# Gates of two feed-forward steps computed together, and a planner that orders shared PSUM reads

## The chip, the cores and the metric

The kernel runs on one core of a Trainium2 chip. The metric is the device time of one execution in microseconds (us). The core has engines that run side by side, each through its own list of instructions in order: TensorE (matmuls into PSUM; PE in the profile, PEld its weight loads), VectorE (DVE), ScalarE (ACT), GpSimd (POOL, hardly used here) and SyncE (SP, which here only issues DMAs).

## The reference

Attention in a sliding window of 64 positions over 8 batches, 8 heads, 576 positions and heads of 64, and behind it a feed-forward layer whose activation is a rational function:

```python
scores = scale * q @ k.T            # only 0 <= rel < 64 counts
attn = softmax(scores)
x = (attn @ v)  ->  [4608 tokens, 512]
h = x @ w_in                        # [4608, 2048]
P = a[0] + a[1] * h + a[2] * h**2 + a[3] * h**3
Q = 1.0 + abs(b[0]) * abs(h) + abs(b[1]) * h**2
out = (P / (Q + 1e-06)) @ w_out     # [4608, 512]
```

## The kernel before, in words

**Tiles and stages.** The tokens are cut into 12 chunks of CH = 384. For a chunk, four attention *units* (one for two heads each; `unit_load`, `unit_scores`, `unit_soft`, `unit_norm`, `unit_transpose`, `unit_av`, lines 402 to 513) produce x, transposed, as a high and a low part. A *step* (c, i) is chunk c and block i of 128 of the 2048 hidden columns; there are 12 x 16 = 192 steps, in the order of `phases` (line 545): the first two chunks take the first half of the blocks and then the second, so that the weights can arrive meanwhile, and all later chunks take 16 blocks in a row.

**A step.** `ffn1` (line 517) multiplies x by a block of w_in: 12 matmuls of 384 columns into one PSUM tensor h, of which there are two in turn. Then comes the gate (lines 529 to 543): ScalarE reads h three times (Square into u, Abs into r, Identity into num), VectorE reads it twice (num times h, then num plus a1, times h); after that h is free. From u, r and num alone follow u (the denominator less one), Ln and Exp on ScalarE (its reciprocal, in r), the quotient gh, rounded for TensorE, and the remainder gl, through u, u and gl on VectorE. `ffn2` (line 550) multiplies gl and gh by blocks of w_out: nine matmuls of 512 columns into the three PSUM tensors o. It stands LAG = 3 steps behind `ffn1`, and its first matmul reads gl. The rings: r, u and num two tiles each, gh and gl GB = 4 each.

**Weights.** `load_weight` (line 370) turns one staged load w_st into a high and a low part: ScalarE writes top, VectorE puts c (tile w_c) together, ScalarE casts c to the high part, VectorE subtracts to the low part. The loads pass through six spare slots and then a ring of SLOTS = 3; after each conversion `fetch` issues the next load.

**The order of the work.** Nothing runs in the order in which it is written. Every call is recorded by a `Planner` (lines 51 to 226) with a cost, an issue time (`occ`) and a latency (`own`), and the operations it must follow by overlap of what they read and write. `plan` (line 183) then plays a list schedule: the engine that can start first takes, of its operations that are ready, the one that was recorded first. The instructions are emitted in the order of these planned starts, which fixes each engine's list; the waits between engines follow from the emitted order. Because all instructions come out of `emit`, they all stand at line 226 in the profile, and one goes by the names of tiles. `fill` (line 210) puts warming matmuls into gaps that TensorE has before the first use of o.

**Attention units.** The scores go into the PSUM pair ps_s; in chunks up to ON_PE = 2 the mask is added by TensorE, later by VectorE. The softmax is written to sm (ring of two), multiplied by the reciprocal sums on VectorE, transposed by TensorE into ps_s, and copied to pT (one tile) by ScalarE. The products with v go to ps_x. The loads qk and vt have rings of two.

Of the kernel before, what the change touches and what calls it, by code (L numbers as in the profile page):

```python
# [9 lines left out]
F32 = mybir.dt.float32  # L10
# [11 lines left out]
CH = 384  # L22
# [3 lines left out]
LAG = 3  # L26
GB = 4
SLOTS = 3
WARM = 7
FILL = 430  # L30
C1AT = 0, 0, 1, 3
ON_PE = 2
# [18 lines left out]
class Planner:  # L51
# [4 lines left out]

    def __init__(self, nc, free, shares):
        self.nc, self.shares = nc, shares
        self.ops, self.group_op = [], None
        self.free = dict(free)  # L60
        self.hist, self.known, self.loads = {}, {}, []
        for name, engine in dict(vector="DVE", scalar="ACT", tensor="PE", gpsimd="POOL", sync="SP").items():
            setattr(self, name, Recorder(self, engine, getattr(nc, name)))
# [46 lines left out]
    def cost(self, engine, method, out, reads, kw, args):  # L110
        if isinstance(out, Late):
            n = out.size // 4
        else:
            n = 1
            for _, k in out.ap[1:]:
                n *= k
        if engine == "SP":
            parts = 128 if isinstance(out, Late) else (out.ap[0][1] if out.tensor.__class__.__name__ != "DRamTensorHandle" else 0)
            size = mybir.dt.size(out.dtype) * n * (parts or out.ap[0][1])
            return 400, 400, size  # L120
        if engine == "PE":
            if method == "transpose":
                return 109, 270, 0
            if isinstance(args[2], Late):
                n = args[2].size // 4
            else:
                n = 1
                for _, k in args[2].ap[1:]:
                    n *= k
                if args[2].dtype == F32:  # L130
                    return (45, 270, 0) if args[1].ap[0][1] == 64 else (52, 225, 0)
            return n * 0.452, n * 0.452 + 165, 0
        if engine == "ACT":
            if "accum_out" in kw:
                return 343, 450, 0
            f = args[2] if len(args) > 2 else None
            occ = 58 + 0.813 * n
            if n == 512:
                occ = 640 if method == "copy" and getattr(out, "dtype", None) == F16 else 510
            for k in ("scale", "bias"):  # L140
                if isinstance(kw.get(k), bass.AP):
                    occ += 92
            if f in (AF.Ln, AF.Exp):
                occ += 55
            return occ, occ + 120, 0
        if engine == "DVE":
            if method == "tensor_reduce":
                n = 1
                for _, k in reads[0].ap[1:]:
                    n *= k  # L150
            if n < 16:
                return 90, 185, 0
            occ = 65 + 1.045 * n
            if isinstance(kw.get("scalar"), bass.AP):
                occ += 62
            return occ, occ + 85, 0
        if engine == "POOL":
            return (n * 2.0 + 60, n * 2.0 + 100, 0) if method in ("tensor_scalar", "tensor_copy") else (n * 2.4 + 130, n * 2.4 + 170, 0)

    def add(self, op):  # L160
        op.index, op.before, op.after = len(self.ops), set(), []
        op.ready = max([self.known.get(name, 0) for name, *_ in op.reads + op.writes], default=0)
        for is_write, spans in ((False, op.reads), (True, op.writes)):
            for name, p0, p1, b0, b1 in spans:
                for q0, q1, c0, c1, other, wrote in self.hist.get(name, ()):
                    if (wrote or is_write) and p0 < q1 and q0 < p1 and b0 < c1 and c0 < b1:
                        op.before.add(other)
# [6 lines left out]
        for wrote, spans in ((False, op.reads), (True, op.writes)):  # L174
            for name, p0, p1, b0, b1 in spans:
                h = self.hist.setdefault(name, [])
                if wrote:
                    h[:] = [x for x in h if not (p0 <= x[0] and x[1] <= p1 and b0 <= x[2] and x[3] <= b1)]
                h.append((p0, p1, b0, b1, op.index, wrote))
                if name in self.shares:  # L180
                    self.hist.setdefault(self.shares[name], []).append((0, 128, 0, 1 << 20, op.index, False))

    def plan(self):
# [6 lines left out]
        for _ in self.ops:  # L190
            start, engine = min((max(self.free[e], min(o.ready for o in w)), e) for e, w in waiting.items() if w)
            op = min((o for o in waiting[engine] if o.ready <= start), key=lambda o: o.index)
            waiting[engine].remove(op)
# [35 lines left out]
class Recorder:  # L229
# [3 lines left out]
    def __getattr__(self, method):  # L233
        return lambda *args, **kw: self.planner.record(self.engine, self.owner, method, args, kw)


# [11 lines left out]
def swa_rational_ffn(ctx: ExitStack, tc: tile.TileContext, qk, v, w_in, w_out, out):  # L248
# [56 lines left out]

    warm = const.tile([P, 512], BF16, name="warm")
    nc.vector.memset(warm, 0.0)
    for _ in range(WARM):
        nc.tensor.matmul(ps_o[2], warm[:, 0:P], warm, start=True, stop=True)
    make_mask()  # L310
# [28 lines left out]
    UNIT = QKAB + TC * P  # L339
    qk_ring = Ring(ring, 2, [P, QKAB], F32, "qk")  # L340
    vt_ring = Ring(ring, 2, [P, TC * P], F32, "vt")
    w_ring = Ring(ring, SLOTS, [P, 1026], F32, "w_st")
    spare = [late.tile([P, H * NCC * P], F32, name=f"early_{n}", tag=f"late_{n}") for n in ("wi_h", "wi_l")]
    spare_slots = [t[:, k * 1026:(k + 1) * 1026] for k in range(H * NCC * P // 1026) for t in spare]
    c_ring = Ring(ring, 2, [P, 512], F32, "w_c")
    top_ring = Ring(const, 0, [], F32, "top")
    top_ring.tiles = tops
    sm_ring = Ring(ring, 2, [P, 2, PR, P], F32, "sm")
    pT_ring = Ring(ring, 1, [P, 2, PR * P], F32, "pT")
    small = {n: Ring(ring, 2, [P, 2 * PR], F32, n) for n in ("nmx", "sums", "rs")}  # L350
    tmp = {n: Ring(ring, 2, [P, CH], F32, n) for n in ("r", "u", "num")}
    g_ring = [Ring(ring, GB, [P, CH], F32R, n) for n in ("gh", "gl")]
    ob_ring = Ring(ring, 2, [P, DO], F32, "ob")

    shares = {t.tensor.name: f"late_{n}" for t, n in zip(early + spare, ("wo_l", "wo_h", "wi_h", "wi_l"))}
    pl = Planner(nc, dict(DVE=4700, ACT=2100, PE=WARM * 430 + 1200, POOL=5000, SP=750), shares)
    pl.ready_at(mask, 4300)
# [12 lines left out]
    def load_weight(which, i):  # L370
        w = staged.pop((which, i))
        f = (lambda t: t.rearrange("p c n -> p (c n)")) if which == "in" else (lambda t: t)
        hi_name, lo_name = ("wi_h", "wi_l") if which == "in" else ("wo_h", "wo_l")
        top, c = top_ring(), c_ring()
        low = w.bitcast(U32)[:, 0:1024].rearrange("p (n two) -> p n two", two=2)[:, :, 1]
# [13 lines left out]
    def load_qk(c, hp):  # L389
        qk_t = early[hp // 2][:, hp % 2 * UNIT:hp % 2 * UNIT + QKAB] if c == 0 else qk_ring()  # L390
        pl.sync.dma_start(out=qk_t, in_=qk[hp, c])
# [48 lines left out]
    def score_maximum(c, hp):  # L440
        u = live[c, hp]
        on_pe, ps, both, m = u["on_pe"], u["ps"], u["both"], u["m"]
        sm, nmx = u["sm"], u["nmx"] = sm_ring(), small["nmx"]().rearrange("p (z r) -> p z r", z=2)
        if not on_pe:
# [30 lines left out]
    def unit_transpose(c, hp):  # L475
        u = live[c, hp]
        ps, both = two_banks(c, hp, True)
        with pl.group():
            for j in range(2 * PR):
                pl.tensor.transpose(ps[j // PR][:, (j % PR) * P:(j % PR + 1) * P], u["sm"][:, j, :], ident)  # L480
        pT = u["pT"] = pT_ring()
        if both is not None:
# [33 lines left out]

    def ffn1(c, i):
        h = h_ring()[:, 0:CH]
        n = 0
# [3 lines left out]
        with whole:  # L523
            for cc in range(NCC):
                with pl.group():
                    for w, x in (("wi_h", 1), ("wi_h", 0), ("wi_l", 0)):
                        pl.tensor.matmul(h, weight_piece(w, i, cc), x_sb[x_slot(c)][x][cc], start=n == 0, stop=n == 3 * NCC - 1)
                        n += 1
        r, u, num = (tmp[n]() for n in ("r", "u", "num"))
        gh, gl = (g() for g in g_ring)  # L530
        pl.scalar.activation(u, h, AF.Square)
        pl.scalar.activation(r, h, AF.Abs, scale=b_raw[:, 0:1])
        pl.scalar.activation(num, h, AF.Identity, scale=a_sb[:, 3:4], bias=a_sb[:, 2:3])
        pl.vector.scalar_tensor_tensor(out=u, in0=u, scalar=b_sb[:, 1:2], in1=r, op0=ALU.mult, op1=ALU.add)
        pl.scalar.activation(r, u, AF.Ln, bias=QADD)
        pl.scalar.activation(r, r, AF.Exp, scale=-1.0)
        pl.vector.tensor_tensor(out=num, in0=num, in1=h, op=ALU.mult)
        pl.vector.scalar_tensor_tensor(out=num, in0=num, scalar=a_sb[:, 1:2], in1=h, op0=ALU.add, op1=ALU.mult)
        pl.vector.scalar_tensor_tensor(out=gh, in0=num, scalar=a_sb[:, 0:1], in1=r, op0=ALU.add, op1=ALU.mult)
        pl.vector.scalar_tensor_tensor(out=u, in0=u, scalar=QADD, in1=gh.bitcast(F32), op0=ALU.add, op1=ALU.mult)  # L540
        pl.vector.scalar_tensor_tensor(out=u, in0=num, scalar=a_sb[:, 0:1], in1=u, op0=ALU.add, op1=ALU.subtract)
        pl.vector.tensor_tensor(out=gl, in0=u, in1=r, op=ALU.mult)
        gs[c, i] = gh, gl

    phases = [(0, 0, H), (1, 0, H), (1, H, NF), (0, H, NF)] + [(c, 0, NF) for c in range(2, NCH)]
    steps = [(c, i) for c, i0, i1 in phases for i in range(i0, i1)]
    total = len(steps)
    part = {}

    def ffn2(s):  # L550
# [89 lines left out]
    for s in range(total + LAG):  # L640
# [3 lines left out]
        if s < total:  # L644
            ffn1(*steps[s])
        for fn, *args in todo.get(s, ()):
# [4 lines left out]
    pl.plan()  # L651
    pl.fill("PE", ps_o[2].tensor.name, FILL, (nc.tensor.matmul, (ps_o[2], warm[:, 0:P], warm), dict(start=True, stop=True)))
    pl.emit()
# [37 lines left out]
```

## Time and profile before

| | us |
|---|---|
| median of 3 runs | 982.18 (982.14 to 982.31) |
| the profiled execution | 982.07 |
| its span, first to last instruction | 980.3 |
| TensorE busy | 952.6 (97%) |
| VectorE busy | 911.2 (93%) |
| ScalarE busy | 698.5 (71%) |
| DMA queue, share of 16 engines | 20.2% |

A row of a group reads: line, engine, operation, what it writes <- what it reads, shape, count | busy time in us, mean ns of one | idle time of the engine just before these instructions, and what ended it. A row of the timeline reads: start in us, length in us, engine, line, operation, tiles. Matmuls overlap: one takes 0.33 to 0.40 us in the rows, but the next one starts after 0.17 us (384 columns) or 0.23 us (512 columns). VectorE's and ScalarE's rows overlap a little as well, so what an instruction costs its engine is read from start to start. A row of the waits reads: who waited <- for whom: us in total, times, longest.

### The profile page before, as it was taken

The numbers are of one execution on the slowest core, as the hardware profiler recorded it, in microseconds if no ns is written. First come the engines' busy times: TensorE is split into PE (matmuls) and PEld (weight loads), VectorE is DVE, ScalarE is ACT, GpSimd is POOL, SyncE is SP. The second block draws the span as 40 slices with busy tenths as digits, with TensorE's granted clock in tenths as the row PEclk, the third lists the DMA queues.
The fourth block names the chain that finished last, engine by engine and source line by source line (L and its number), as shares of the span: only waits on it lengthen the run. The fifth ranks groups of instructions, "written<-read, shape, count | busy, mean of one in ns | idle before, by whom it ended". The sixth has DMA issues, their size and how long they took to land.

```text
span 980.3 us, 17701 instructions
## 1 busy us (share of the span) xinstructions
PE 952.6 (97%) x6672; PEld 824.6 (84%) x6675; DVE 911.2 (93%) x1747; ACT 698.5 (71%) x1737; POOL 4.4 (0%) x20
## 2 busy tenths in 40 slices
PE   8899999999999999999999999999999999999998
PEld 5677788888888888888888888888888888888996
DVE  6999999998999999999999999999999899999996
ACT  7988777776667667767677677667766776676664
POOL 1000000000000000000000000000000000000000
PEclk9999999999999999999999999999999999999999
DMA  9344341313103103103102200210310310300000
GB/s 360 127 171 147 122 150 39 96 50 117 51 1 117 35 17 118 35 17 116 37 17 74 79 17 26 93 51 1 118 35 17 118 35 18 100 1 2 33 1 32
DMA packets 24564, 68.38 MB, mean 70 GB/s; under 512 B 2720, under 2 KB 2720, under 8 KB 24480
## 3 DMA queue, kind: packets, MB, share of 16 engines
q1 hardware_dynamic: 24480, 67.27, 20.2%
q8 instruction: 52, 0.85, 0.4%
q14 instruction: 32, 0.26, 0.1%
HBM read 57.03 MB, written 10.22 MB: 69 GB/s over the span
## 4 chain that ended last, share of the span: by engine, by line
PE 64%; DVE 19%; ACT 10%; issue 2%; DMA 1%; ACTq 0%; DVEq 0%
PE o L226 29%; PE h L226 28%; DVE u L226 6%; PE ps_s L226 5%; ACT sm L226 4%; DVE num L226 3%; PE ps_x L226 3%; ACT r L226 2%; DVE gh L226 2%; DVE sm L226 2%; DVE nmx L226 1%; ACT u L226 1%; DVE gl L226 1%; DMA w_st<-w_out 1%; ACT num L226 1%
## 5 line engine op out<-in xcount | busy, mean ns | idle before, releaser
L226 PE MATMUL h<-xl,wi_h 128*128 128x384 f32 x768 | 260.4, 339 | 7.7 <-DVE num L226 6.2
L226 PE MATMUL h<-xh,wi_l 128*128 128x384 f32 x768 | 258.1, 336 | 0.0
L226 PE MATMUL h<-xh,wi_h 128*128 128x384 f32 x768 | 257.9, 336 | 0.0
L226 PE MATMUL o<-wo_h,gl 128*128 128x512 f32 x576 | 236.5, 411 | 2.5 <-DVE gl L226 1.7
L226 PE MATMUL o<-wo_h,gh 128*128 128x512 f32 x576 | 228.2, 396 | 0.0
L226 PE MATMUL o<-wo_l,gh 128*128 128x512 f32 x576 | 227.0, 394 | 0.0
L226 ACT ACTIVATE u<-h 128x384 f32<-128x384 f32 x192 | 94.2, 491 | 158.4 <-PE h L226 153.6
L226 PEld LDWEIGHTS h<-xl,wi_h 128*128 128x128 f32 x768 | 144.2, 188 | 20.3 <-DVE num L226 10.2
L226 PEld LDWEIGHTS h<-xh,wi_h 128*128 128x128 f32 x768 | 144.2, 188 | 7.2
L226 ACT ACTIVATE num<-h,ab_sb 128x384 f32<-128x384 f32 x192 | 129.7, 675 | 25.7 <-PE h L226 15.6
L226 PEld LDWEIGHTS h<-xh,wi_l 128*128 128x128 f32 x768 | 144.2, 188 | 0.3 <-DVE wi_l L226 0.3
L226 ACT ACTIVATE r<-u 128x384 f32<-128x384 f32 x192 | 101.3, 527 | 48.1 <-DVE u L226 44.8
L226 PEld LDWEIGHTS o<-wo_h,gl 128*128 128x128 f32 x576 | 108.1, 188 | 29.0 <-issue 5.1
L226 PEld LDWEIGHTS o<-wo_h,gh 128*128 128x128 f32 x576 | 108.5, 188 | 26.3
L226 DVE SCALAR_TENSOR_TENSOR gh<-num,ab_sb,r 128x384 fp32r<-128x384 f32 x192 | 117.9, 614 | 8.7 <-ACT r L226 1.6
L226 PEld LDWEIGHTS o<-wo_l,gh 128*128 128x128 f32 x576 | 108.7, 189 | 16.5
L226 DVE SCALAR_TENSOR_TENSOR num<-num,ab_sb,h 128x384 f32<-128x384 f32 x192 | 117.3, 611 | 5.6 <-ACT r L226 1.5
L226 DVE SCALAR_TENSOR_TENSOR u<-u,b_sb,r 128x384 f32<-128x384 f32 x192 | 117.9, 614 | 2.9 <-ACT r L226 1.0
L226 DVE SCALAR_TENSOR_TENSOR u<-num,ab_sb,u 128x384 f32<-128x384 f32 x192 | 118.1, 615 | 2.7
L226 ACT ACTIVATE r<-h,ab_sb 128x384 f32<-128x384 f32 x192 | 111.4, 580 | 11.1 <-DVE num L226 11.1
L226 DVE SCALAR_TENSOR_TENSOR u<-u,gh 128x384 f32<-128x384 f32 x192 | 106.4, 554 | 2.7
L226 DVE TENSOR_TENSOR num<-num,h 128x384 f32<-128x384 f32 x192 | 105.0, 549 | 3.5 <-ACT r L226 2.2
(74 smaller groups left out, 983.6 us busy)
## 6 DMA issues: line engine op xcount, KB each, us to landing
qk<-qk SPq DMA_DIRECT2D x44, 419.0 KB, 4.2
vt<-v SPq DMA_DIRECT2D x44, 384.0 KB, 3.6
out<-ob SPq DMA_DIRECT2D x33, 256.0 KB, 2.1
w_st<-w_out SPq DMA_DIRECT2D x15, 512.0 KB, 3.5
w_st<-w_in SPq DMA_DIRECT2D x11, 512.0 KB, 3.6
early<-qk SPq DMA_DIRECT2D x4, 419.0 KB, 5.5
early<-v SPq DMA_DIRECT2D x4, 384.0 KB, 8.1
early_wi_l<-w_in SPq DMA_DIRECT2D x3, 512.0 KB, 9.4
```

The costliest lines, as they stand in the source:

```text
L226: call(*[value(x) for x in args], **{k: value(x) for k, x in kw.items()})
```

## The change

Steps are put in groups: the first four and the last four alone, all others two by two (92 pairs). `ffn1` now only makes h; a new function `gate` runs when the last step of its group has its h. Both h tensors of a pair are taken when the pair begins. The reads of h stay one by one for each step (three on ScalarE, two on VectorE); everything behind them, u, Ln, Exp, gh, u, u and gl, is one instruction for both steps, on tiles with two halves. The tiles come from `Slots`: TMP = 6 double tiles for num, u and r together, two double tiles each for gh and gl. LAG stays 3.

```diff
-        r, u, num = (tmp[n]() for n in ("r", "u", "num"))
-        gh, gl = (g() for g in g_ring)
-        pl.scalar.activation(u, h, AF.Square)
-        pl.scalar.activation(r, h, AF.Abs, scale=b_raw[:, 0:1])
-        pl.scalar.activation(num, h, AF.Identity, scale=a_sb[:, 3:4], bias=a_sb[:, 2:3])
+    def gate(group, hs):
+        size = len(group)
+        num, u, r = (tmp(size) for _ in range(3))
+        gh, gl = (g(size) for g in g_ring)
+        for k, h in enumerate(hs):
+            u1, r1, num1 = (t if size == 1 else t[:, k] for t in (u, r, num))
+            pl.scalar.activation(u1, h, AF.Square)
+            pl.scalar.activation(r1, h, AF.Abs, scale=b_raw[:, 0:1])
+            pl.scalar.activation(num1, h, AF.Identity, scale=a_sb[:, 3:4], bias=a_sb[:, 2:3])
+            pl.vector.tensor_tensor(out=num1, in0=num1, in1=h, op=ALU.mult)
+            pl.vector.scalar_tensor_tensor(out=num1, in0=num1, scalar=a_sb[:, 1:2], in1=h, op0=ALU.add, op1=ALU.mult)
         pl.vector.scalar_tensor_tensor(out=u, in0=u, scalar=b_sb[:, 1:2], in1=r, op0=ALU.mult, op1=ALU.add)
         pl.scalar.activation(r, u, AF.Ln, bias=QADD)
         pl.scalar.activation(r, r, AF.Exp, scale=-1.0)
-        pl.vector.tensor_tensor(out=num, in0=num, in1=h, op=ALU.mult)
-        pl.vector.scalar_tensor_tensor(out=num, in0=num, scalar=a_sb[:, 1:2], in1=h, op0=ALU.add, op1=ALU.mult)
         pl.vector.scalar_tensor_tensor(out=gh, in0=num, scalar=a_sb[:, 0:1], in1=r, op0=ALU.add, op1=ALU.mult)
...
+    groups = [[s] for s in range(ALONE[0])] + [[s, s + 1] for s in range(ALONE[0], total - ALONE[1], 2)]
+    groups += [[s] for s in range(total - ALONE[1], total)]
...
+class Slots:
+    def __init__(self, pool, n, shape, dtype, name):
+        self.tiles = [pool.tile([shape[0], 2, *shape[1:]], dtype, name=f"{name}_{k}") for k in range(n)]
+        self.n = 0
+    def __call__(self, size):
+        t, k = self.tiles[self.n // 2 % len(self.tiles)], self.n % 2
+        self.n += size
+        return t if size == 2 else t[:, k]
```

The planner gets the names of the PSUM tensors (`banks`: ps_s, ps_x, the three o and the two h). Any two accesses to one of them by different engines, two reads as well, count as ordered, in the order in which they were recorded. On TensorE it first looks among operations that have been ready for 300 ns (`MARGIN`). Some costs change: a matmul's from 0.452 to 0.4545 ns a column, an exponential with its sum that reads SBUF from 343 to 386 ns, a ScalarE instruction of 512 elements that reads PSUM to 466, a unit's transposes by 50 more.

```diff
+MARGIN = dict(PE=300)
...
-                    if (wrote or is_write) and p0 < q1 and q0 < p1 and b0 < c1 and c0 < b1:
+                    apart = self.ops[other].engine != op.engine
+                    if name in self.banks and apart or (wrote or is_write) and p0 < q1 and q0 < p1 and b0 < c1 and c0 < b1:
...
-            op = min((o for o in waiting[engine] if o.ready <= start), key=lambda o: o.index)
+            able = [o for o in waiting[engine] if o.ready <= start]
+            op = min([o for o in able if o.ready <= start - MARGIN.get(engine, 0)] or able, key=lambda o: o.index)
```

Buffers make room for the double tiles: qk has one tile in its ring instead of two (two loads of chunk 1 lie behind the early loads instead), w_c is gone and the conversion writes into the first half of the staged load itself, pT is gone and the transposed softmax is copied back into sm, and two units of chunk 0 keep sm behind the spare slots. The warming matmuls read a tile of 128 columns four times over instead of one of 512.

```diff
-    qk_ring = Ring(ring, 2, [P, QKAB], F32, "qk")
+    qk_ring = Ring(ring, 1, [P, QKAB], F32, "qk")
...
-        top, c = top_ring(), c_ring()
+        top, c = top_ring(), w[:, 0:512]
...
-        pT = u["pT"] = pT_ring()
+        pT = u["pT"] = u["sm"].rearrange("p (z r) c -> p z (r c)", z=2)
...
+        elif c == 1 and hp < 2:
+            qk_t = early[hp][:, 2 * UNIT:2 * UNIT + QKAB]
...
+        if c == 0 and hp >= 2:
+            sm = spare[hp - 2][:, SPARES * 1026:SPARES * 1026 + 2 * PR * P].rearrange("p (z r c) -> p z r c", z=2, c=P)
```

More of the change, by code (lines that the diff above doesn't have):

```diff
@@ L26 @@
 LAG = 3
-GB = 4
+PAIRS = 2, 2
+TMP = 6
+ALONE = 4, 4
 SLOTS = 3
@@ L55, with __init__ @@
     DMA_LANES = 8
-    def __init__(self, nc, free, shares):
+    def __init__(self, nc, free, shares, banks):
         self.nc, self.shares = nc, shares
         self.ops, self.group_op = [], None
-        self.free = dict(free)
+        self.free, self.banks = dict(free), set(banks)
         self.hist, self.known, self.loads = {}, {}, []
@@ L131, in cost @@
                     return (45, 270, 0) if args[1].ap[0][1] == 64 else (52, 225, 0)
-            return n * 0.452, n * 0.452 + 165, 0
+            return n * 0.4545, n * 0.4545 + 165, 0
         if engine == "ACT":
             if "accum_out" in kw:
-                return 343, 450, 0
+                return (343, 450, 0) if reads[0].tensor.name in self.banks else (386, 490, 0)
             f = args[2] if len(args) > 2 else None
@@ L139, in cost @@
                 occ = 640 if method == "copy" and getattr(out, "dtype", None) == F16 else 510
+                if reads[0].tensor.name in self.banks:
+                    occ = 466
             for k in ("scale", "bias"):
@@ L176, in add @@
                 h = self.hist.setdefault(name, [])
-                if wrote:
+                if wrote and name not in self.banks:
                     h[:] = [x for x in h if not (p0 <= x[0] and x[1] <= p1 and b0 <= x[2] and x[3] <= b1)]
@@ L304, in swa_rational_ffn @@
     b_sb = const.tile([P, 2], F32, name="b_sb")
-    warm = const.tile([P, 512], BF16, name="warm")
+    warm = const.tile([P, P], BF16, name="warm")
     nc.vector.memset(warm, 0.0)
+    warm_up = (ps_o[2], warm, warm.unsqueeze(1).broadcast_to([P, 4, P]))
     for _ in range(WARM):
-        nc.tensor.matmul(ps_o[2], warm[:, 0:P], warm, start=True, stop=True)
+        nc.tensor.matmul(*warm_up, start=True, stop=True)
     make_mask()
@@ L343, in swa_rational_ffn @@
     spare = [late.tile([P, H * NCC * P], F32, name=f"early_{n}", tag=f"late_{n}") for n in ("wi_h", "wi_l")]
-    spare_slots = [t[:, k * 1026:(k + 1) * 1026] for k in range(H * NCC * P // 1026) for t in spare]
-    c_ring = Ring(ring, 2, [P, 512], F32, "w_c")
+    SPARES = H * NCC * P // 1026
+    spare_slots = [t[:, k * 1026:(k + 1) * 1026] for k in range(SPARES) for t in spare]
     top_ring = Ring(const, 0, [], F32, "top")
@@ L348, in swa_rational_ffn @@
     sm_ring = Ring(ring, 2, [P, 2, PR, P], F32, "sm")
-    pT_ring = Ring(ring, 1, [P, 2, PR * P], F32, "pT")
     small = {n: Ring(ring, 2, [P, 2 * PR], F32, n) for n in ("nmx", "sums", "rs")}
-    tmp = {n: Ring(ring, 2, [P, CH], F32, n) for n in ("r", "u", "num")}
-    g_ring = [Ring(ring, GB, [P, CH], F32R, n) for n in ("gh", "gl")]
+    tmp = Slots(ring, TMP, [P, CH], F32, "tmp")
+    g_ring = [Slots(ring, n, [P, CH], F32R, name) for n, name in zip(PAIRS, ("gh", "gl"))]
     ob_ring = Ring(ring, 2, [P, DO], F32, "ob")
     shares = {t.tensor.name: f"late_{n}" for t, n in zip(early + spare, ("wo_l", "wo_h", "wi_h", "wi_l"))}
-    pl = Planner(nc, dict(DVE=4700, ACT=2100, PE=WARM * 430 + 1200, POOL=5000, SP=750), shares)
+    pl = Planner(nc, dict(DVE=4700, ACT=2100, PE=WARM * 430 + 1200, POOL=5000, SP=750), shares, [t.tensor.name for t in [ps_s, ps_x, *ps_o, *h_ring.tiles]])
     pl.ready_at(mask, 4300)
@@ L389, in load_qk @@
     def load_qk(c, hp):
-        qk_t = early[hp // 2][:, hp % 2 * UNIT:hp % 2 * UNIT + QKAB] if c == 0 else qk_ring()
+        if c == 0:
+            qk_t = early[hp // 2][:, hp % 2 * UNIT:hp % 2 * UNIT + QKAB]
+        elif c == 1 and hp < 2:
+            qk_t = early[hp][:, 2 * UNIT:2 * UNIT + QKAB]
+        else:
+            qk_t = qk_ring()
         pl.sync.dma_start(out=qk_t, in_=qk[hp, c])
@@ L442, in score_maximum @@
         on_pe, ps, both, m = u["on_pe"], u["ps"], u["both"], u["m"]
-        sm, nmx = u["sm"], u["nmx"] = sm_ring(), small["nmx"]().rearrange("p (z r) -> p z r", z=2)
+        if c == 0 and hp >= 2:
+            sm = spare[hp - 2][:, SPARES * 1026:SPARES * 1026 + 2 * PR * P].rearrange("p (z r c) -> p z r c", z=2, c=P)
+        else:
+            sm = sm_ring()
+        nmx = small["nmx"]().rearrange("p (z r) -> p z r", z=2)
+        u["sm"], u["nmx"] = sm, nmx
         if not on_pe:
@@ L477, in unit_transpose @@
         ps, both = two_banks(c, hp, True)
-        with pl.group():
+        with pl.group(50):
             for j in range(2 * PR):
                 pl.tensor.transpose(ps[j // PR][:, (j % PR) * P:(j % PR + 1) * P], u["sm"][:, j, :], ident)
-        pT = u["pT"] = pT_ring()
+        pT = u["pT"] = u["sm"].rearrange("p (z r) c -> p z (r c)", z=2)
         if both is not None:
@@ L515, in swa_rational_ffn, with ffn1 @@
     gs = {}
-    def ffn1(c, i):
-        h = h_ring()[:, 0:CH]
+    def ffn1(c, i, h):
         n = 0
@@ L542, in ffn1 @@
         pl.vector.tensor_tensor(out=gl, in0=u, in1=r, op=ALU.mult)
-        gs[c, i] = gh, gl
+        for k, s in enumerate(group):
+            gs[steps[s]] = (gh, gl) if size == 1 else (gh[:, k], gl[:, k])
     phases = [(0, 0, H), (1, 0, H), (1, H, NF), (0, H, NF)] + [(c, 0, NF) for c in range(2, NCH)]
@@ L548, in swa_rational_ffn @@
     part = {}
+    groups = [[s] for s in range(ALONE[0])] + [[s, s + 1] for s in range(ALONE[0], total - ALONE[1], 2)]
+    groups += [[s] for s in range(total - ALONE[1], total)]
+    group_of = {s: g for g in groups for s in g}
     def ffn2(s):
@@ L644, in swa_rational_ffn @@
         if s < total:
-            ffn1(*steps[s])
+            group = group_of[s]
+            if s == group[0]:
+                hs = [h_ring()[:, 0:CH] for _ in group]
+            ffn1(*steps[s], hs[s - group[0]])
+            if s == group[-1]:
+                gate(group, hs)
         for fn, *args in todo.get(s, ()):
@@ L651, in swa_rational_ffn @@
     pl.plan()
-    pl.fill("PE", ps_o[2].tensor.name, FILL, (nc.tensor.matmul, (ps_o[2], warm[:, 0:P], warm), dict(start=True, stop=True)))
+    pl.fill("PE", ps_o[2].tensor.name, FILL, (nc.tensor.matmul, warm_up, dict(start=True, stop=True)))
     pl.emit()
```

## The prediction

> **What bounds the kernel now.** I read the page's head first, then the busy time of each engine by stage, then the groups of TensorE's instructions with what ended their idle time.
>
> ```profile
> span 980.3 us, 17701 instructions
> PE 952.6 (97%) x6672; PEld 824.6 (84%) x6675; DVE 911.2 (93%) x1747; ACT 698.5 (71%) x1737; POOL 4.4 (0%) x20
> ```
>
> The table by stage (columns: length, then busy time and count of PE, PEld, DVE, ACT, POOL, then clock, DMA share, GB/s):
>
> ```profile
> 20.00:80.00 60.00, 52.27 (x459) 40.90 (x459) 58.73 (x115) 55.91 (x144) 0.00 (x0) 1.00 0.46 170
> 80.00:150.00 70.00, 65.44 (x336) 55.69 (x335) 69.77 (x134) 55.33 (x113) 0.00 (x0) 1.00 0.41 132
> 150.00:240.00 90.00, 87.40 (x679) 74.46 (x678) 83.27 (x165) 63.98 (x175) 0.00 (x0) 1.00 0.26 82
> 240.00:960.00 720.00, 715.48 (x4947) 630.53 (x4948) 674.06 (x1283) 502.74 (x1242) 0.00 (x0) 1.00 0.14 47
> ```
>
> There are two kernels in one. Up to 150 us VectorE is the limit: it is busy for 128.5 of the 130 us between 20 and 150, because it unpacks weights beside the gates, and TensorE is idle for 7.7 + 4.6 us. From 240 us on TensorE is the limit, idle for 4.5 of 720 us, and VectorE has 46 us to spare. Between them lies a stage with 2.6 us of idle TensorE. Whatever the change does to VectorE counts in full before 150 us and hardly at all after 240 us. All idle time of TensorE from 20 to 960 us together is 19.4 us: more than that can't be won without taking matmuls away, and the change takes none away.
>
> What ended that idle time, first over 80 to 150 us, then over 240 to 960 us (last column: idle before, and the releaser):
>
> ```profile
> L226 PE MATMUL h<-xl,wi_h 128*128 128x384 f32 x59 | 20.6, 349 | 4.1 <-DVE num L226 4.1
> ```
>
> ```profile
> L226 PE MATMUL h<-xl,wi_h 128*128 128x384 f32 x596 | 200.3, 336 | 0.0
> L226 PE MATMUL ps_s<-ident,sm 128*128 128x128 f32 x204 | 28.7, 277 | 4.9 <-ACT ob L226 2.7 <-DVE sm L226 2.2
> ```
>
> Early, the first ffn product waits for VectorE's last read of h: backlog. Late, only the transposes of the attention unit wait, for VectorE's product sm or a copy beside it. The 596 matmuls are four to a step: 149 steps in 720 us, 4.83 us a step.
>
> **The change, part by part.** *Merged instructions.* From step 4 on, five VectorE instructions of a gate (two u, gh, u minus, gl) and Ln and Exp of ScalarE run once for two steps on 768 elements. What that saves is the fixed part, read from start to start in VectorE's timeline where it has a queue of ready work:
>
> ```profile
> 256.76 0.96 DVE L226 TENSOR_TENSOR sm<-sm,rs 128x768 f32<-128x768 f32 x1
> 257.64 0.61 DVE L226 SCALAR_TENSOR_TENSOR gh<-num,ab_sb,r 128x384 fp32r<-128x384 f32 x1
> 258.17 0.61 DVE L226 SCALAR_TENSOR_TENSOR u<-u,b_sb,r 128x384 f32<-128x384 f32 x1
> 258.70 0.55 DVE L226 SCALAR_TENSOR_TENSOR u<-u,gh 128x384 f32<-128x384 f32 x1
> 259.17 0.55 DVE L226 TENSOR_TENSOR num<-num,h 128x384 f32<-128x384 f32 x1
> ```
>
> 768 elements take 0.88 us, 384 take 0.47 us, and 0.53 us where a scalar is read from a tile. So two instructions of 0.47 become one of 0.88 (0.06 saved, twice a pair), and two of 0.53 become one of 0.94 (0.12, three times): 0.48 us of VectorE a pair. How many pairs lie in the stage where that counts:
>
> ```profile
> L226 DVE TENSOR_TENSOR gl<-u,r 128x384 fp32r<-128x384 f32 x18 | 10.0, 555 | 0.0
> ```
>
> This row (the last instruction of each gate) is for 62 to 150 us, in which the gates of steps 4 to 21 end. 18 steps, 9 pairs: 9 x 0.48 = **4.3 us less** before 150 us; bounds 0 and the 12.3 us that TensorE is idle there. I take the whole 4.3, since VectorE has no gap there into which the saving could vanish. The Trainium skill (Perfetto Trace Analysis, Optimizing Scalar/DVE Operations) puts the fixed cost on VectorE at about 60 ns an instruction and says that grouping pays where the engine is saturated; by its figure this term would be 5 x 0.06 x 9 = 2.7 us, an estimate. The rows agree for the instructions without a scalar from a tile, and give twice as much for the others.
>
> From 150 to 240 us, at 4.83 us a step, nine more pairs save 4.3 us of VectorE, but it has 6.7 us of gaps there already; of the 2.6 us that TensorE loses I take **1.5 us less** (bounds 0 and 2.6). After 240 us the merging itself is worth nothing: TensorE's matmuls cover it. ScalarE's saving is worth nothing anywhere (idle 28% of the span). Its size, for the latency below:
>
> ```profile
> 256.99 0.51 ACT L226 ACTIVATE r<-r 128x384 f32<-128x384 f32 x1
> 257.40 0.56 ACT L226 ACTIVATE r<-h,ab_sb 128x384 f32<-128x384 f32 x1
> ...
> 259.25 0.78 ACT L226 COPY pT<-ps_s 128x768 f32<-128x768 f32 x1
> 259.93 0.53 ACT L226 ACTIVATE r<-r 128x384 f32<-128x384 f32 x1
> ```
>
> 0.41 us becomes about 0.41 + 0.32, since the 768 copy takes 0.68.
>
> *The new order.* The late stalls are planning errors. One of them:
>
> ```profile
> 449.34 0.39 ACT L226 ACTIVATE sm<-sm,nmx 128x128 f32<-128x128 f32 x1
> ...
> 449.72 0.39 ACT L226 ACTIVATE sm<-sm,nmx 128x128 f32<-128x128 f32 x1
> ...
> 450.59 0.33 PE L226 MATMUL h<-xh,wi_h 128*128 128x384 f32 x1
> ...
> 450.67 0.96 DVE L226 TENSOR_TENSOR sm<-sm,rs 128x768 f32<-128x768 f32 x1
> 450.76 0.34 PE L226 MATMUL h<-xh,wi_l 128*128 128x384 f32 x1
> ...
> 451.77 0.85 PE L226 MATMUL ps_s<-ident,sm 128*128 128x128 f32 x6 [0.68 <-ACT ob L226]
> ```
>
> The transposes start 1.01 us after the last matmul, which itself started 0.17 us after the one before it. They stand in the queue too early: the planner books 343 ns for each exponential and its sum, the trace shows 380, and six of them make sm late by 0.2 us, with the product behind it. The new costs book 386, and MARGIN lets TensorE prefer work that was ready 300 ns ago. The booked sequence on PSUM tensors costs nothing itself. I take **4.0 us less** of the 4.9 in the row above (bounds 0 and 4.9).
>
> *Buffers.* The weight conversion now writes its intermediate w_c into the staged load itself, so a slot is given back after the two instructions that follow, not before them:
>
> ```profile
> SPq L226 <- DVE w_c L226: 81.8, 20, 8.4
> ```
>
> ```profile
> L226 ACT CAST wi_h<-w_c 128x512 fp32r<-128x512 f32 x16 | 10.1, 637 | 0.6 <-DVE w_c L226 0.3
> L226 DVE TENSOR_TENSOR wi_l<-w_c,wi_h 128x512 fp32r<-128x512 f32 x16 | 10.9, 689 | 0.5 <-ACT wi_h L226 0.5
> ```
>
> ```profile
> ACT top L226 <- DMA w_st<-w_out: 1.5, 2, 0.8
> ```
>
> The DMA queue already waits for such a slot 20 times, and each will come 0.64 + 0.69 = 1.33 us later. Behind that wait SP holds later weights, qk and v. But ScalarE, which opens a load, came to wait for a landing only twice, 1.5 us in all. Bounds: 0, and 20 x 1.33 = 27 us. The near row is the two waits; I take one of them passed on: **1.3 us more**. The qk ring of one tile: a load now waits for the previous unit's scores, and
>
> ```profile
> qk<-qk SPq DMA_DIRECT2D x44, 419.0 KB, 4.2
> ```
>
> 4.2 us fit between units that come every four steps, 4 x 4.83 = 19.3 us (two steps, 9.7 us, in chunk 2): I take nothing, and 4.2 us for each unit whose cover goes. The Trainium skill (Trainium Kernel Development and Optimization, Best Practices) asks for double buffers; by that rule this ring is wrong, and the case where it costs is in the second rival. pT inside sm, smaller warm tile, first and last four steps alone: nothing, as their orders are those of before (bounds of 0.3 us either way by the last stages' unchanged work).
>
> The sum: -4.3 - 1.5 - 4.0 + 1.3 = -8.5 us on the profiled execution's 982.07 us (span 980.3 and 1.8 around it; 0.1 under the median of 982.18): **973.6 us**.
>
> **The rivals.** *The pair is too slow for its first step (slower).* One late step of before, from the last matmul of its h to the first use of its gl:
>
> ```profile
> 525.05 0.34 PE L226 MATMUL h<-xh,wi_l 128*128 128x384 f32 x1
> ```
>
> ```profile
> 528.45 0.61 DVE L226 SCALAR_TENSOR_TENSOR num<-num,ab_sb,h 128x384 f32<-128x384 f32 x1
> ...
> 532.90 0.55 DVE L226 TENSOR_TENSOR gl<-u,r 128x384 fp32r<-128x384 f32 x1
> ```
>
> ```profile
> 529.41 0.33 PE L226 MATMUL h<-xl,wi_h 128*128 128x384 f32 x1
> ...
> 540.21 0.50 PE L226 MATMUL o<-wo_h,gl 128*128 128x512 f32 x1
> ```
>
> h ends at 525.39, gl at 533.45, and it is used at 540.21: 6.8 us of slack. In a pair the first step waits 4.83 us for the second h, and its chain holds five VectorE and two ScalarE instructions that are longer by 0.41 and 0.32: 2.7 us. 6.8 - 4.8 - 2.7 = -0.7. TensorE must then run a product of h ahead, which it may when that h is read out; here the last read ends at 529.06 and the tensor is written again at 529.41, so the room is 0.35 us. If it fails in one pair out of two (those beside an attention unit), 37 units after 240 us lose 0.7 us: +26 - 8.5 = 999.6 us, 990 to 1010. It decides from a loss of 0.11 us a pair (the 9.8 us of gains over 92 pairs). For it: the numbers above. Against it: two h first, then two second products, is an order that gives both the chain and h a whole second product more room, and the planner, which works with these latencies, is free to choose it, as its queue picks whatever is ready. The Trainium skill (Perfetto Trace Analysis, the same section) adds that where these engines are not saturated but cause bubbles, instructions should be broken up, not grouped; after 240 us this kernel is such a place, and this rival is what that rule would do. Chance 0.13.
>
> *Slots come back late.* If ten of the 20 loads land late by the full 1.33 us, +13 replaces the 1.3: 985 us, 980 to 990; it beats the gains from eight loads on, and a late qk load behind them would add its 4.2. For it: SP's 81.8 us; against: ScalarE's two waits. Chance 0.09, half of it within 0.2%.
>
> *Only the early part.* The late stalls move elsewhere: 982.07 - 4.3 + 1.3 = 979.1 and up to 1.5 less: 977.5 to 979. Chance 0.18. *Nearly all idle time goes:* 963 to 967 (19.4 less is 962.7). Chance 0.13. *The change doesn't do what it says:* the two halves of a pair stay interleaved with waits such that nothing is saved: 982. Chance 0.05.
>
> **How the numbers follow.** The forecast, 968 to 977 with 973.6 as its sum, has 0.42. Faster by over 0.2% (2 us, about what a measurement can tell) are the forecast, the early part only, and nearly all: 0.42 + 0.18 + 0.13 = 0.73. Within 0.2%: 0.05 + 0.04 = 0.09. Slower: 0.13 + 0.05 = 0.18. The range runs from 963 to 987: it leaves out the pair's rival (0.13), a tail of late slots (0.02) and the far end of the best case (0.03).
>
> **What would show it.** Right: 92 merged rows each with 128x768 for u, gh and gl near 1.0 us; VectorE's busy time down by about 44 us (92 x 0.48), yet the span by only 9; the first product of step 22 starting about 4 us before its 142.23, in this row; the idle time before ps_s<-ident under 1 us after 240 us.
>
> ```profile
> 142.23 0.34 PE L226 MATMUL h<-xl,wi_h 128*128 128x384 f32 x1
> ```
>
> Wrong: idle time before o<-wo_h,gl released by DVE gl, or before h released by DVE num, in the late stage (the first rival); ScalarE's top waiting for DMA w_st (the second); the same 4.9 us of late idle time in other rows (only the early part).

## The result, and the profile after

The changed kernel takes 972.83 us (median of 4 runs, 972.32 to 973.52) where the kernel before, beside it on the same chip, takes 982.16: a ratio of 0.9906, 95% interval 0.9891 to 0.9921. The forecast was 973.6 us, so the total came out as predicted. Its terms did not: up to the mark used below the change gave 1.8 us, where the terms for that part add up to 4.5 (4.3 + 1.5 - 1.3), and behind it 6.8, where 4.0 were forecast. Two errors of nearly the same size cancelled, and that was luck.

The head of the page of after:

```profile
span 971.7 us, 16840 instructions
PE 948.9 (98%) x6673; PEld 829.1 (85%) x6673; DVE 856.8 (88%) x1287; ACT 665.9 (69%) x1553; POOL 4.4 (0%) x20
```

VectorE has 460 instructions less, five for each of the 92 pairs, and 54 us of busy time (44 were expected from start to start; two rows of 0.61 us become one of 1.0). The span fell by 8.6 us. The busy time by stage (columns as in the prediction):

```profile
20.00:80.00 60.00, 48.56 (x428) 38.80 (x429) 56.73 (x106) 53.45 (x135) 0.00 (x0) 0.94 0.50 170
80.00:150.00 70.00, 67.63 (x353) 59.07 (x352) 69.04 (x101) 54.48 (x104) 0.00 (x0) 1.00 0.37 125
150.00:240.00 90.00, 88.88 (x689) 76.32 (x689) 77.84 (x118) 60.06 (x156) 0.00 (x0) 1.00 0.25 82
240.00:960.00 720.00, 719.92 (x4986) 639.59 (x4985) 635.42 (x924) 482.02 (x1101) 0.00 (x0) 1.00 0.14 47
```

After 240 us TensorE is idle for 0.1 of 720 us, where it was 4.5. Between 20 and 80 us it is idle for 11.4 us, where it was 7.7: that stage got worse. Over the three stages from 20 to 240 us together its idle time is the same in both kernels, 14.9 us. The first matmul of step 48 (the first product of chunk 3) marks where the weights and chunk 2 are behind; in the timeline of before and of after it stands at

```profile
277.94 0.34 PE L226 MATMUL h<-xl,wi_h 128*128 128x384 f32 x1
```

```profile
276.17 0.34 PE L233 MATMUL h<-xl,wi_h 128*128 128x384 f32 x1
```

So 1.8 us of the gain lie before that mark, and 6.8 behind it (980.3 - 277.94 = 702.36 us of the span before, 971.7 - 276.17 = 695.53 after). The mark is good to about 2 us, since orders differ there by up to one second product.

The largest new loss in the early part is one wait. TensorE's timeline of after around it:

```profile
66.75 0.40 PE L233 MATMUL o<-wo_h,gh 128*128 128x512 f32 x1
72.56 0.66 PE L233 MATMUL ps_s<-ident,sm 128*128 128x128 f32 x2 [5.42 <-DVE sm L233]
```

```profile
73.73 0.78 PE L233 MATMUL o<-wo_h,gl 128*128 128x512 f32 x1
74.30 0.63 PE L233 MATMUL o<-wo_l,gh 128*128 128x512 f32 x1
74.73 0.63 PE L233 MATMUL o<-wo_h,gh 128*128 128x512 f32 x1
```

and VectorE's, which has no gap in it:

```profile
71.47 0.95 DVE L233 TENSOR_TENSOR sm<-sm,rs 128x768 f32<-128x768 f32 x1
72.33 0.95 DVE L233 TENSOR_TENSOR gl<-tmp,tmp 128x768 fp32r<-128x768 f32 x1
73.20 1.01 DVE L233 TENSOR_TENSOR tmp<-tmp,h 128x384 f32<-128x384 f32 x2
74.13 1.13 DVE L233 SCALAR_TENSOR_TENSOR tmp<-tmp,ab_sb,h 128x384 f32<-128x384 f32 x2
```

At 67 us everything that TensorE could do waits for VectorE: the transposes for sm (done at 72.4), the second product of the first paired step for gl (73.3), and the next product of h for a free h, both of which the next pair holds until VectorE's last read of them (from 74.1 on).

### The profile page after: what moved, and what is told of

It reads as the page before. It is cut to its first block, busy times and chain, and to the rows that moved or that the text cites. A ratio compares the mean times of both kernels' runs of the same rounds, so it can differ in the third digit from the quotient of the medians.

```text
span 971.7 us, 16840 instructions
## 1 busy us (share of the span) xinstructions
PE 948.9 (98%) x6673; PEld 829.1 (85%) x6673; DVE 856.8 (88%) x1287; ACT 665.9 (69%) x1553; POOL 4.4 (0%) x20
## 4 chain that ended last, share of the span: by engine, by line
PE 88%; DVE 8%; ACT 3%; issue 1%; DMA 1%; SPq 0%; ACTq 0%; DVEq 0%
PE o L233 40%; PE h L233 38%; PE ps_s L233 6%; PE ps_x L233 4%; DVE tmp L233 3%; ACT tmp L233 1%; DVE gh L233 1%; DMA early_wi_h<-w_in 1%; DVE w_st L233 1%; DVE wi_l L233 1%; DVE gl L233 0%; DVE sm L233 0%; ACT sm L233 0%; DVE nmx L233 0%; DVE wo_l L233 0%
## 5 line engine op out<-in xcount | busy, mean ns | idle before, releaser
L233 ACT ACTIVATE tmp<-h 128x384 f32<-128x384 f32 x192 | 94.3, 491 | 233.1 <-PE h L233 232.8
L233 ACT ACTIVATE tmp<-h,ab_sb 128x384 f32<-128x384 f32 x384 | 221.0, 629 | 2.4 <-PE h L233 2.4
L233 ACT ACTIVATE tmp<-tmp 128x768 f32<-128x768 f32 (+1 forms) x200 | 164.6, 823 | 20.6 <-DVE tmp L233 17.8
L233 DVE SCALAR_TENSOR_TENSOR gh<-tmp,ab_sb,tmp 128x768 fp32r<-128x768 f32 (+1 forms) x100 | 98.2, 982 | 54.4 <-ACT tmp L233 54.0
L233 DVE SCALAR_TENSOR_TENSOR tmp<-tmp,ab_sb,h 128x384 f32<-128x384 f32 x192 | 116.9, 610 | 3.0
L233 DVE SCALAR_TENSOR_TENSOR tmp<-tmp,b_sb,tmp 128x768 f32<-128x768 f32 (+1 forms) x96 | 95.8, 998 | 23.9 <-ACT tmp L233 23.8
L233 DVE TENSOR_TENSOR tmp<-tmp,h 128x384 f32<-128x384 f32 x192 | 105.1, 548 | 5.6 <-ACT tmp L233 5.4
L233 DVE SCALAR_TENSOR_TENSOR tmp<-tmp,ab_sb,tmp 128x768 f32<-128x768 f32 (+1 forms) x96 | 95.8, 998 | 1.3
L233 DVE SCALAR_TENSOR_TENSOR tmp<-tmp,gh 128x768 f32<-128x768 f32 (+1 forms) x100 | 92.1, 921 | 1.5
L233 DVE TENSOR_TENSOR gl<-tmp,tmp 128x768 fp32r<-128x768 f32 (+1 forms) x96 | 90.0, 937 | 1.5
```

Of the source, the lines that this page charges most:

```text
L233: call(*[value(x) for x in args], **{k: value(x) for k, x in kw.items()})
```

## The experiments

All times are medians, timed in five rounds beside the kernel before. The idle time is 720 us less TensorE's busy time in the stage from 240 to 960 us. The last two columns are of the profiled execution: where step 48 begins, and what of the span lies behind it.

| kernel | us | ratio to before, 95% | late idle, us | step 48 at | behind it |
|---|---|---|---|---|---|
| before | 982.16 | | 4.5 | 277.9 | 702.4 |
| after | 972.83 | 0.9891 to 0.9921 | 0.1 | 276.2 | 695.5 |
| e1_single | 975.98 | 0.9926 to 0.9953 | 0.7 | 278.6 | 696.6 |
| e2_oldplan | 971.02 | 0.9878 to 0.9905 | 0.1 | 273.7 | 695.8 |
| e3_newplan | 974.24 | 0.9912 to 0.9937 | 2.7 | 273.6 | 699.2 |
| e4_late24 | 972.21 | 0.9891 to 0.9918 | 0.1 | 275.1 | 695.5 |
| e5_single_oldplan | 979.66 | 0.9976 to 0.9993 | 4.8 | 271.4 | 705.4 |
| e6_single_tmp3 | 976.57 | 0.9941 to 0.9966 | 0.9 | 275.9 | 698.8 |
| e7_pairs_old_wc | 981.83 | 0.9997 to 1.0015 | 0.1 | 281.1 | 695.8 |
| e8_inplace | 981.33 | 0.9992 to 1.0009 | 5.4 | 274.2 | 704.9 |
| e9_costs | 976.57 | 0.9935 to 0.9961 | 3.1 | 277.1 | 698.9 |
| e10_margin | 978.21 | 0.9953 to 0.9976 | 3.6 | 275.5 | 700.9 |
| e11_unmerged | 976.93 | 0.9940 to 0.9964 | 0.0 | 282.5 | 695.4 |
| e12_pairs24_old | 971.60 | 0.9885 to 0.9910 | 0.1 | 274.2 | 695.8 |

The kernel before had medians of 981.2 to 981.6 us in the jobs of these twelve.

### Which half makes the late gain: the planner or the pairs?

**e1_single**, every step alone in the changed kernel:

```diff
-    groups = [[s] for s in range(ALONE[0])] + [[s, s + 1] for s in range(ALONE[0], total - ALONE[1], 2)]
-    groups += [[s] for s in range(total - ALONE[1], total)]
+    groups = [[s] for s in range(total)]
```

> The changed kernel with every step alone: new planner and new buffers, no pairs. Order theory (the late gain of 8 us comes from the planner's new order and costs): TensorE's idle time after 240 us stays under 1 us, and the time is 973 to 977 us. Pair theory (it comes from the 44 us that merging takes off VectorE): the late waits before the transposes come back, 4 us or more, and the time is 979 to 983 us.

**e2_oldplan**, pairs and new buffers with the planner of before:

```diff
-MARGIN = dict(PE=300)
+MARGIN = {}
-        self.free, self.banks = dict(free), set(banks)
+        self.free, self.banks = dict(free), set()
...
-                return (343, 450, 0) if reads[0].tensor.name in self.banks else (386, 490, 0)
+                return 343, 450, 0
```

(and the other costs as before)

> The changed kernel with pairs and new buffers but the planner of before (old costs, no margin, no sequence on PSUM tensors). Order theory: late idle time of TensorE of 4 us or more, 978 to 982 us. Pair theory: late idle time under 1.5 us, 972 to 975 us.

**e3_newplan**, the kernel before with the new planner and nothing else:

```diff
+MARGIN = dict(PE=300)
...
-    pl = Planner(nc, dict(...), shares)
+    pl = Planner(nc, dict(...), shares, [t.tensor.name for t in [ps_s, ps_x, *ps_o, *h_ring.tiles]])
```

(and the costs and the order as in the change)

> The kernel before with nothing new but the planner (costs, margin, sequence on PSUM tensors). Order theory: 973 to 977 us, as without pairs in the changed kernel. Pair theory: 980 to 983 us. If this one is slow and the changed kernel without pairs is fast, it is the buffers.

The stage from 240 to 960 us in e2 and in e3:

```profile
240.00:960.00 720.00, 719.92 (x4981) 637.60 (x4980) 637.19 (x923) 480.18 (x1099) 0.00 (x0) 1.00 0.14 47
```

```profile
240.00:960.00 720.00, 717.28 (x4970) 637.26 (x4969) 676.87 (x1293) 503.06 (x1247) 0.00 (x0) 1.00 0.14 47
```

Both theories were right about their own kernel (e2 is 1 us faster still than the pair theory's range), so as rivals both fell: the two halves replace each other. Pairs with the old planner take all of the late idle time away; the new planner without pairs takes 1.8 of 4.5 us away on the kernel before and nearly all on the changed one. Behind step 48 the pairs with the new buffers gain 6.6 us (702.4 to 695.8), the planner alone 3.2, and all together 6.8. The whole time says the same: against the kernel before in their own jobs, the planner alone gains 7.4 us (e3), pairs and buffers alone 10.6 (e2), and all together 9.3. More than half of the planner's 7.4 us lies before step 48 (277.9 to 273.6 in the profiles), where the prediction gave it nothing. What the planner leaves can be seen in the group of the transposes in e3, beside after:

```profile
L231 PE MATMUL ps_s<-ident,sm 128*128 128x128 f32 x198 | 27.1, 273 | 2.7 <-ACT ob L231 2.7
```

```profile
L233 PE MATMUL ps_s<-ident,sm 128*128 128x128 f32 x204 | 27.8, 272 | 0.0
```

### Which part of the pairs, and which of the planner?

**e5_single_oldplan**, e1's and e2's edits together, so that only the buffers are new:

```diff
-    groups = [[s] for s in range(ALONE[0])] + ...
+    groups = [[s] for s in range(total)]
-MARGIN = dict(PE=300)
+MARGIN = {}
```

(and the rest of e2's edit)

> The changed kernel with every step alone and the planner of before: only the new buffers are left (temporaries for four steps instead of two, no own tile for w_c, one qk tile, pT in sm). Depth theory (the late gain comes from temporaries for more steps, which pairs bring with them, and not from merging): idle time of TensorE after 240 us under 1.5 us, and since the early part loses up to 6 us, 976 to 979 us. Merging theory: late idle time of 4 us or more, and 982 to 987 us.

**e6_single_tmp3**, e1 with half the temporaries:

```diff
-TMP = 6
+TMP = 3
```

> The changed kernel with every step alone and half the temporaries (TMP = 3: two steps, as before), with the new planner. Depth theory: late idle time back to about 2.7 us, as the new planner has it on the kernel before, and 978 to 981 us. If depth does nothing: 975 to 977 us, as with every step alone and full depth.

On the idle time and on the whole time the depth theory fell. With the old planner and no pairs the deeper temporaries leave the late wait where it was, now behind the transposes once more in e5:

```profile
L231 PE MATMUL ps_s<-ident,sm 128*128 128x128 f32 x198 | 27.8, 277 | 4.8 <-ACT ob L231 4.7
```

and half the depth costs 0.6 us with the new one, less than the spread of the runs. Behind step 48, though, half the depth does cost 2.2 us (698.8 against 696.6), which an earlier step 48 hides. The new buffers alone lose 3.0 us there (705.4 in e5 against 702.4), so the pairs on top of them, with the same planner, gain 9.6 (695.8 in e2). The merging theory's price for e5 (982 to 987) was too high as well: it took 979.66.

**e9_costs** and **e10_margin**, the kernel before with one part of the new planner each:

```diff
+            return n * 0.4545, n * 0.4545 + 165, 0
+                return (343, 450, 0) if reads[0].tensor.name in self.banks else (386, 490, 0)
```

(and the other new costs)

> The kernel before with the planner's new costs alone (no margin, no sequence on PSUM tensors). If the late waits of before are planning errors in the costs, as the prediction had it, most of the planner's late gain of 3.9 us is here: idle time of TensorE after 240 us of 3 us or less, 976 to 979 us. If the margin makes it: idle time stays at 4 us or more, 980 to 983 us, give or take what a new order does to the first 240 us.

```diff
+            able = [o for o in waiting[engine] if o.ready <= start]
+            op = min([o for o in able if o.ready <= start - MARGIN.get(engine, 0)] or able, key=lambda o: o.index)
```

> The kernel before with the margin alone: TensorE first looks among work ready for 300 ns. If the margin makes the planner's late gain: idle time after 240 us of 3 us or less, 976 to 979 us. If the costs make it: 4 us or more, 980 to 983 us.

Neither expectation was met cleanly: late idle time of 3.1 and 3.6 us, against 4.5 without and 2.7 with everything. Each makes a part of it, the costs somewhat more. Behind step 48 the costs alone gain 3.5 us, the margin alone 1.5, and the whole planner 3.2, so the costs suffice for its late gain. The sequence on PSUM tensors was not run alone.

**e11_unmerged**, the changed kernel with its pairs, and every merged instruction issued as two halves:

```diff
-        pl.vector.scalar_tensor_tensor(out=u, in0=u, scalar=b_sb[:, 1:2], in1=r, op0=ALU.mult, op1=ALU.add)
+        for num1, u1, r1, gh1, gl1 in whole:
+            pl.vector.scalar_tensor_tensor(out=u1, in0=u1, scalar=b_sb[:, 1:2], in1=r1, op0=ALU.mult, op1=ALU.add)
```

(and so for all seven)

> The changed kernel with its pairs, but every merged instruction issued as two, one for each step, so that the grouping stays and only the merging is undone. Throughput theory (the prediction's early term): VectorE works 44 us more, the stage up to 150 us loses 4.3 us, 976 to 979 us. If the merging only gives slack that the late stage does not need once the new planner is there: 971 to 974 us.

```profile
240.00:960.00 720.00, 720.00 (x4992) 640.16 (x4991) 661.25 (x1298) 495.50 (x1260) 0.00 (x0) 1.00 0.14 48
```

The stage from 240 to 960 us in e11, above, separates the two things that a pair is. After 240 us the grouping alone, with the new planner, is as good as the merged pairs: TensorE has no idle time at all. (Grouping without merging was not run with the planner of before.) The merging is worth 976.93 - 972.83 = 4.1 us, and it lies before step 48, where the throughput theory put it: behind that mark e11 loses nothing. (The mark itself, 282.5 against 276.2, says 6.3 us, but the profiled execution of e11 was the slowest of its six, 979.72 us.) The six spread from 975.31 to 979.72 us, and the two slowest had the lowest granted clock (0.994, where the two fastest had 0.998 and 0.999), so the 4.1 us is good to about 2 us. Nor is it throughput alone. From 80 to 150 us VectorE is busy for only 65.1 of 70 us in e11 (69.0 in after), and TensorE waits longer for gl (over 20 to 150 us, in e11, then in after):

```profile
80.00:150.00 70.00, 60.33 (x296) 51.27 (x295) 65.12 (x123) 48.72 (x97) 0.00 (x0) 0.95 0.38 125
```

```profile
PE o L233 <- DVE gl L233: 8.2, 6, 2.4
```

```profile
PE o L233 <- DVE gl L233: 2.7, 3, 1.1
```

e1 and e11 differ in the grouping alone. It costs 0.95 us in all (975.98 to 976.93), which is less than e11's spread, although it gains 1.2 us behind step 48.

### Why the early part did not gain

**e4_late24**, pairs from step 24 on:

```diff
-ALONE = 4, 4
+ALONE = 24, 4
```

> The changed kernel with pairs only from step 24 on, after the weights. If early pairs cause the wait of 5.4 us before the transposes at 72 us (the first step of a pair too late, both h taken), it goes, and the time is 965 to 969 us. If the weights stage is bound by VectorE's throughput, as the prediction had it, the lost merging costs 4.3 us: 976 to 978 us.

Neither number was met: 972.21 us. At the place of after's wait, e4 has

```profile
70.37 0.34 PE L233 MATMUL h<-xh,wi_l 128*128 128x384 f32 x1
70.96 0.85 PE L233 MATMUL ps_s<-ident,sm 128*128 128x128 f32 x6 [0.25 <-DVE sm L233]
```

The 5.42 us are 0.25: with steps alone an h was free, and TensorE ran products of h until sm was ready. So the pairs cause that wait. With the planner of before it is the same: e2, with pairs from step 4, has

```profile
PE ps_s L231 <- DVE sm L231: 4.6, 1, 4.6
```

and e12 below, with pairs from step 24, has no wait for VectorE's sm there. It seems to take the merged instructions as well: e11 has the pairs unmerged, and no wait of TensorE longer than 2.4 us. But other waits come instead (over 20 to 150 us, in e4, then in after):

```profile
PE h L233 <- DVE tmp L233: 8.9, 7, 1.9
```

```profile
PE h L233 <- DVE tmp L233: 3.8, 3, 1.6
```

VectorE is the limit of this stage either way (busy for 127.9 of the 130 us in e4, 125.8 in after); e4 has lost the merging there and got rid of the wait, and in sum the two are worth the same. **e12_pairs24_old** asks that once more with the planner of before, and whether the best early and the best late part add up:

```diff
-ALONE = 4, 4
+ALONE = 24, 4
```

(on e2)

> The changed kernel with the planner of before and pairs only from step 24 on: its first part is planned as in the kernel with every step alone and the planner of before (4.8 us ahead of before at 240 us), its late part as in the one with pairs and that planner (7.6 us gained after 240 us). If the two parts add up: 982 - 12.4 = 969 to 970 us, faster than both kernels and than every run so far. If pairs are worth something before 150 us too: 971 us or more.

971.60 us against 971.02 with pairs from step 4, within the spread of the runs. The parts did not add up: step 48 begins 2.8 us later than in e5, with the steps from 24 on in pairs. With both planners, pairs before step 24 are worth nothing that can be measured (0.6 us slower, 0.6 us faster).

### The slots

**e8_inplace**, the kernel before with w_c in the staged load:

```diff
-        top, c = top_ring(), c_ring()
+        top, c = top_ring(), w[:, 0:512]
```

> The kernel before with w_c written into the staged load, nothing else. The prediction's term: 1.3 us more, 982.5 to 984 us. Slot theory: 3 to 6 us more, 985 to 988 us. If slots don't matter: 981 to 982 us.

**e7_pairs_old_wc**, e2 with one tile w_c of its own again:

```diff
+    c_ring = Ring(ring, 1, [P, 512], F32, "w_c")
-        top, c = top_ring(), w[:, 0:512]
+        top, c = top_ring(), c_ring()
```

> The changed kernel with pairs, the planner of before, and w_c again a tile of its own (one, not two), so that a slot is free after two instructions of the conversion. Slot theory (the early loss comes from slots given back late): the wait at 72 us shrinks, and it is 966 to 969 us, faster than both. Pair latency theory (the first step of a pair comes too late there): the wait stays, 970 to 972 us.

The slot theory fell on the kernel before, where late slots cost nothing (ratio 0.9992 to 1.0009). In the changed kernel, giving them back early made e2 slower by 10.8 us, which met neither expectation. But e7 is no clean opposite: there is room for one tile only, so a conversion must wait for the one before it, and its early waits are of another kind (over 20 to 150 us):

```profile
PE o L231 <- DVE gl L231: 10.7, 6, 3.9
```

Which of its two changes makes the 10.8 us was not separated.

## Why the prediction was right in sum and wrong in its terms

**Merged instructions, -4.3 us early.** The size of the saving was right, the net was not. The saving of each instruction is as computed: in after's late timeline

```profile
252.07 1.01 DVE L233 SCALAR_TENSOR_TENSOR tmp<-tmp,ab_sb,tmp 128x768 f32<-128x768 f32 x1
253.00 0.60 DVE L233 SCALAR_TENSOR_TENSOR tmp<-tmp,ab_sb,h 128x384 f32<-128x384 f32 x1
253.53 0.95 DVE L233 TENSOR_TENSOR gl<-tmp,tmp 128x768 fp32r<-128x768 f32 x1
254.39 0.16 DVE L233 TENSOR_SCALAR sums<-sums 128x6 f32<-128x6 f32 x1
```

the merged forms take 0.93 and 0.86 us from start to start (0.94 and 0.88 were expected). Undoing the merging costs 4.1 us (e11); that this is so near to 4.3 is partly luck, since e11 loses by late results as well and not by throughput alone. The step that failed is "I take the whole 4.3, since VectorE has no gap there into which the saving could vanish": the term counted the merging and not the grouping that comes with it. Shown is that pairs before step 24 are worth nothing in sum (e4, e12), and that the 5.42 us wait comes and goes with them (e4). The first product of step 24 starts at the same time in before and in after:

```profile
151.73 0.34 PE L226 MATMUL h<-xl,wi_h 128*128 128x384 f32 x1
```

```profile
151.81 0.42 PE L233 MATMUL h<-xl,wi_h 128*128 128x384 f32 x1
```

How the loss is shared out between the wait, the slow matmuls behind it and other late results was not separated.

**The first rival** (the pair too slow for its first step, both h taken) was the right mechanism at the wrong place. It was priced after 240 us, where it does not happen: no idle time is left there, with merged pairs or unmerged. It happens in the weights stage, where VectorE's backlog makes the chain far longer than the late step that was measured. The rival's own sign, TensorE's idle time before gl, stands there in e11 (8.2 us) and e7 (10.7), where before has 1.7. A hint could have been read in before, where TensorE's largest early wait is the one of h for DVE num (6.2 us over 20 to 150). In its working, the 0.32 us for ScalarE does not follow from the copy of 0.68 us that it names (0.68 - 0.41 = 0.27), but it came out nearly so: in after a merged form takes 0.75 us. The Trainium skill (Perfetto Trace Analysis, Optimizing Scalar/DVE Operations) says that grouping can improve throughput where the engine is saturated, and that breaking up may let work finish sooner where it is not but causes bubbles. The first agrees with e11, which loses 4.1 us by breaking up, and loses it before step 48. For the second no difference shows: after 240 us merged and broken-up pairs leave 0.1 and 0.0 us of idle time.

**The new order, -4.0 us late.** The size was off, and half of the reason. Behind step 48 the gain is 6.8 us. The planner alone gives 3.2 us of it, and its costs alone suffice for that (e9), as the prediction had it. But pairs with the new buffers give 6.6 without the planner, and the prediction gave them nothing there. "After 240 us the merging itself is worth nothing" holds with the new planner (e11); it left out what the grouping does. The idle time that the page showed before the transposes (4.9 us) was taken as the upper bound, and the gain behind step 48 went past it, because idle time is counted only where the modelled end of a matmul lies before the next start: the quoted stall counts 0.68 us, but the start came 1.01 us after the last one, where 0.17 is usual. Counted from start to start against the usual spacing, TensorE loses some 7 us less from 240 to 960 us in after than in before (an estimate from the two traces), where the idle time fell by 4.4. Why grouping helps there is argued, not shown: in after, VectorE stands idle before gh for ScalarE's Exp,

```profile
L233 DVE SCALAR_TENSOR_TENSOR gh<-tmp,ab_sb,tmp 128x768 fp32r<-128x768 f32 (+1 forms) x78 | 77.8, 998 | 48.1 <-ACT tmp L233 47.9
```

so that sm's product finds it free; but e11, with more work on VectorE, has no late wait either.

**150 to 240 us, -1.5 us,** looks met, since TensorE's idle time there fell from 2.6 to 1.1 us. But e3 has 0.5 us there without any pairs, and e8 has 1.5, so this does not show that the merging did it, and the term can't be told apart from the rest of the early part. Its bound is how much any new order moves that part: e8, whose median does not move at all, has step 48 at 274.2 instead of 277.9 us and loses it again later, and e5 has it at 271.4. A single profile differs there by 3.7 us for an edit that leaves the median where it was.

**Slots, +1.3 us.** By e8 the term is nothing on the kernel before. The second rival goes with it, though in after ScalarE's waits for staged loads rose from 1.5 to 3.2 us over 20 to 150 us, as that rival said they would: waits of an engine that is not the limit.

**What would have shown it wrong** did its work: the first product of step 22 was to come 4 us sooner and came 1.6 us sooner,

```profile
140.63 0.41 PE L233 MATMUL h<-xl,wi_h 128*128 128x384 f32 x1
```

which says that the early term had failed, while the sum was right.

No version beats the changed kernel clearly. e2, e12 and e4 have lower medians (971.0, 971.6 and 972.2), with intervals that overlap its own.

## What to carry to other kernels

Merging the work of two steps has two effects: it saves the fixed part of each instruction, and it holds every buffer of the first step until the second is there. Price both in the stage where the engine is saturated, because there the longer holding can starve the next engine just where the saving would count. And where two parts of a change are aimed at the same few microseconds of idle time, they replace each other instead of adding up; only runs with each of them alone can tell.

## What the runs showed of the hardware

After the wait of 5.42 us TensorE came back slow: the matmuls of 512 columns follow each other after 0.43 us (73.73 aside, 74.30, 74.73 in the rows above), where 0.23 is usual, and the table by stage gives a granted clock of 0.50 for 72.5 to 78 us:

```profile
72.50:78.00 5.50, 5.44 (x36) 4.36 (x36) 4.29 (x7) 1.57 (x2) 0.00 (x0) 0.50 0.33 98
```

5.5 us at half the clock lose up to 2.75 us, so this stall cost up to half as much again. In before no wait of TensorE between 20 and 150 us is longer than 1.4 us, and the clock stayed at 1.00.

Shorter waits can do it too. In e1 the clock fell behind a wait of 1.87 us:

```profile
82.85 0.45 PE L233 MATMUL h<-xl,wi_h 128*128 128x384 f32 x1 [1.87 <-DVE tmp L233]
```

```profile
84.10:87.50 3.40, 3.40 (x11) 3.10 (x10) 3.40 (x7) 2.68 (x7) 0.00 (x0) 0.50 0.25 80
```

It fell behind 1.84 us in e10 and 2.44 us in e9 as well, while a second wait of 1.87 us in e1 and one of 1.90 us in e4 left it at 1.00. So the length of a wait does not decide alone, and what else does is not shown. The Trainium skill (TensorE: Matmul & The Clock Gate, Part 1) has the clock fall to half after an idle window of some 3.4 us. The wait of 5.42 us agrees with that; those in e1, e9 and e10 were shorter, and here the runs decide.
